# A polysketch attention feeding a SwiGLU block: key features of the third batch earlier, query features one operation per unit, weight splits later

## The chip, the cores and the metric

The kernel runs on one core of a Trainium2 chip. The metric is the device time of one execution in microseconds (us), as the median of the runs given. The profile is of one further execution, with its own time.

## The reference

Four batches of four heads, 1088 tokens of 32 numbers each. Attention has no softmax: queries and keys are turned into 64 products of two sketches of 8, keys and values are summed once per head, and every query is a product with that sum. The result (4352 tokens of 128 numbers) goes through a SwiGLU block with 1536 hidden numbers.

```python
def phi(x):
    a = np.einsum('rd,bhsd->bhsr', S1, x)
    b = np.einsum('rd,bhsd->bhsr', S2, x)
    return np.einsum('bhsi,bhsj->bhsij', a, b).reshape(*x.shape[:-1], r * r)
q_p, k_p = (phi(q), phi(k))
kv = np.einsum('bhsf,bhsd->bhfd', k_p, v)
z = np.sum(k_p, axis=2)
num = np.einsum('bhsf,bhfd->bhsd', q_p, kv)
den = np.einsum('bhsf,bhf->bhs', q_p, z)[..., None] + 1e-06
x = (num / den)          # (B,H,S,D) -> (B*S, H*D) = (4352, 128)
g = x @ w_gate           # 128 -> 1536
silu = g * (1.0 / (1.0 + np.exp(-g)))
out = silu * (x @ w_val) @ w_out
```

The inputs come in 64-bit floating point; the kernel makes 32-bit numbers of their words.

## The kernel before

The tokens lie in `xT` (128 x 4352), one column per token, and are cut into blocks: three of the first batch (384, 320, 384 tokens: blocks 0, 1, 2) and then blocks of 480 (3 and on). The hidden numbers are cut into 12 chunks of 128. A *unit* (i, j) is one block by one chunk: a gate product and a value product on PE (TensorE), a Silu on ACT (ScalarE), and a product of the two on DVE (VectorE), which leaves the hidden numbers of the unit in a slot of `hbuf` or `late`. A *down* multiplies one unit's hidden numbers with its chunk of `w_out` and adds to the block's sum in PSUM. The order of work on every engine is the order in which the program issues it: scheduling is by hand, and each engine works through its own queue in that order.

There are two kinds of units. For blocks 0, 1 and part of 2, `unit` (L1010) multiplies 32-bit numbers directly. A unit called with `late=True` does not use DVE: ACT writes Silu to `room` (L1022) and copies the value product to its slot (L1030), and the two are multiplied later on POOL (GpSimd) by `catch_up` (L1039, L1042). Otherwise DVE multiplies them at once (L1033). From unit (2, 6) on, `start_unit` (L976) and `finish_unit` (L987) work with numbers that are split in parts: `start_unit` multiplies the parts `wd` and `xd` (L982) into one of three pairs of PSUM banks and ACT rescales the pair (L985); `finish_unit` adds two more products each (L994, L995), then come Silu (L997) on ACT and the product (L1002) on DVE, after which the pair is free for a later `start_unit`.

The parts of the weights are made by `cut_weights` (L841), for three chunks at a time, in four steps: a rounded copy on ACT (L845), the rest on POOL (L848), a scaled copy of it on ACT (L850), a difference on POOL (L857). In the code `g0` is the gate weights of chunks 0 to 2, `v1` the value weights of chunks 3 to 5, and so on; `at("g0")` issues the next step. `cut_tokens` (L859) makes `x1` on ACT (L867), `xd` (L875) and `x0` (L870) of a block's tokens. `narrow` (L245) makes 32-bit weights out of the words: two operations on DVE, two on ACT (L268, L269), two on DVE (L271, L277), one on POOL (L286); `part("wv", 2)` issues the next of these steps for the value weights of chunks 3 to 5.

The attention of the first batch runs at the start: `query_products`, `query_copy` (L461), `query_features` (`phq`, L475), `totals` (L497) and `divide` (L518 to L539, which writes `xT`). The other batches are a generator, `attentions`, of which `parts_of(n)` runs the next n pieces between units or downs, up to a piece marked "pe" that `group()` runs at a fixed place in the last loop. Its pieces for a batch are: turns of keys and queries (L327, L578); key features `phk` on DVE (`features`, L377); their sums `zs` on POOL (`feature_sums`, L547, five operations); products of features and values (L388), of the next batch's keys (L354) and of the sums (L715) on PE; `fold` (L601 to L608), which puts the sum into the weights `s123`; the queries' sketches with these on PE (L342) and their copies on ACT (L590); `query_step` (L739), eight pieces: `dot` and `den` (L743, L746), the division (L748 to L750), and three times a product `phq` (L377, 768 elements) and its turn into `phT` (L760); and `numerators` (L768), whose products (L778) are copied into `xT` (L795). `phk` and `phT` share one buffer, so the key features of the third batch (index 2) can be written only when the second batch's numerators have been multiplied.

The downs between the last direct unit and unit (2, 6) are the loop over n from 0 to 12; then come units (2, 6) to (2, 11) with a down each (the loop over j), then the remaining downs (`while todo`), and then the last loop over y, 12 units for each of the blocks 3 and on. At y = 4 its first `group()` runs the third batch's sums.

Of the kernel before, what the change touches and what calls it, by code (L numbers as in the profile page):

```python
# [19 lines left out]
def kernel(  # L20
# [28 lines left out]
    nc = tc.nc  # L49
# [263 lines left out]
    late = const.tile([P, NL, BW], FP32, tag="late", name="late", bufs=1)  # L313
# [301 lines left out]
    def attentions():  # L615

        yield from turn_keys(1)
        kp = pair("keys")  # L620
        for i, c in enumerate(kpieces):
            key_products(kp[:, i, :], *c)
        ka = apool.tile([P, NC * H, R], FP32, tag="kas", name="kas")

        def sketch(ps, i):
            c0, c1 = kpieces[i]
            return ps[:, i, 0 : 64 * (c1 - c0)].rearrange("p (x t r) -> p x t r", t=2, r=R)

        for i, (c0, c1) in enumerate(kpieces):
            nc.scalar.copy(ka[:, H * c0 : H * c1, :], sketch(kp, i)[:, :, 0, :])  # L630
        yield from turn_queries(1)
        phk = apool.tile([P, NC, H, R, R], FP32, tag="phk", name="phk")
        for n, (i, c0, c1) in enumerate(((0, 0, 3), (0, 3, 5), (1, 5, 7), (1, 7, 9))):
            first = H * (c0 - kpieces[i][0])
            kb = sketch(kp, i)[:, first : first + H * (c1 - c0), 1, :]
            key_features(phk, (ka[:, H * c0 : H * c1, :], kb), c0, c1)
            if n == 0:
                zs, sums = feature_sums(phk)
            else:
                sums.pop(0)()  # L640
            if n == 3:
                let_go("keys")
            if n % 3 != 1:
                yield
        sums.pop(0)()
        yield from turn_keys(2)
        kvz = pair("values")
        key_values(kvz[:, 0, 0:F], phk, 0, NC)
        kab, copies = sketched(pair(), key_products, 2, "kab2")
        run_copies(copies, 2)  # L650
        value_sums(kvz[:, 0, :], zs)
        fold(kvz[:, 0, :])
        spread = spread_out(1, kvz[:, 0, :])
        let_go("values")
        yield
        qab, copies = sketched(pair(), query_sketches, 3, "qab")
        run_copies(copies, 2)
        yield
        for n, _ in enumerate(query_step(1, qab)):
            if n % 2 == 1:  # L660
                yield
        numerators(1, spread)
        yield "first"

        phk = apool.tile([P, NC, H, R, R], FP32, tag="phk", name="phk")
        yield from features(phk, kab)
        zs, sums = feature_sums(phk)
        for f in sums:
            f()
        yield from turn_keys(3)  # L670
        yield from turn_queries(2)
        for b in (2, 3):
            yield "pe"
            if b == 3:
                numerators(2, spread)
            kv = bank("g2")
            key_values(kv[:, 0:F], phk, 0, NC)
            if b == 2:
                kab, copies = sketched(pair(), key_products, 2, "kab2")
                run_copies(copies, 2)  # L680
            value_sums(kv, zs)
            fold(kv)
            spread = spread_out(b, kv)
            yield
            yield "pe"
            qab, copies = sketched(pair(), query_sketches, 3, "qab")
            run_copies(copies, 2)
            yield
            if b == 2:
                yield from turn_queries(3)  # L690
                phk = late[:, NL - 6 :, :].rearrange("p s (n h i j) -> p (s n) h i j", h=1, i=R, j=R)
                phk = phk.rearrange("p (c h) o i j -> p c (h o) i j", h=H)
                yield from features(phk, kab)
                zs, sums = feature_sums(phk)
            yield from beside(query_step(b, qab), sums)
        yield "pe"
        numerators(3, spread)
        yield
# [40 lines left out]
    def query_step(b, qab):  # L739
        phT = turned[b] = apool.tile([P, H, 2, NC, 32], FP32, tag="phk", name="phT")  # L740
        dot = apool.tile([P, NC * H, R], FP32, tag="dot", name="dot")
        den = apool.tile([P, NC * H], FP32, tag="den", name="den")
        nc.vector.tensor_tensor(  # L743
            out=dot[:], in0=qab[:, 1, :, :], in1=qab[:, 2, :, :], op=ALU.mult
        )
        nc.vector.tensor_reduce(out=den[:], in_=dot[:], axis=AX.X, op=ALU.add)  # L746
        yield
        nc.vector.tensor_scalar_add(den[:], den[:], 1e-6)  # L748
        nc.vector.reciprocal(den[:], den[:])
        nc.vector.tensor_tensor(  # L750
            out=qab[:, 0, :, :], in0=qab[:, 0, :, :],
            in1=den[:].unsqueeze(2).to_broadcast([P, NC * H, R]), op=ALU.mult,
        )
        yield
        for c0, c1 in fpieces:
            x, n = slice(H * c0, H * c1), c1 - c0
            phq = apool.tile([P, NC // 3, H, R, R], FP32, tag="phqs", name="phq")
            key_features(phq, (qab[:, 0, x, :], qab[:, 1, x, :]), 0, n)
            yield
            nc.vector.transpose(  # L760
                out=phT[:, :, :, c0:c1, :].rearrange("p h g c t -> p c (h g) t"),
                in_=phq[:, 0:n, :, :, :].rearrange(
                    "p c h (g i) j -> p c (h g) (i j)", g=2
                ),
            )
            yield
# [32 lines left out]
    HEAD = len(steps)  # L799
    hidden = {}  # L800
    acc = {}
    todo = []
# [207 lines left out]
    def unit(i, j, late=False, between=(None, None), apart=False):  # L1010


        t0, n = blocks[i]
        g, u = halves(pair()) if apart else (bank(), bank())
        for o, w in ((g, wg), (u, wv)):
            if between[0] and w is wv:
                between[0]()
            nc.tensor.matmul(  # L1018
                o[:, 0:n], w[:, j, :], xT[:, t0 : t0 + n], start=True, stop=True
            )  # L1020
        sg = room[:, len(lates) + caught[0], :] if late else fpool.tile([P, WB], FP32, tag="sg", name="sg", bufs=5)
        nc.scalar.activation(sg[:, 0:n], g[:, 0:n], AF.Silu)  # L1022
        slot_of[i, j] = slots.pop(0)
        hj = slot_of[i, j]
        hidden[i, j] = hj
        todo.append((i, j))
        if late:
            if between[1]:
                between[1]()
            nc.scalar.copy(hj[:, 0:n], u[:, 0:n])  # L1030
            lates.append((hj[:, 0:n], sg[:, 0:n]))
        else:
            nc.vector.tensor_tensor(  # L1033
                out=hj[:, 0:n], in0=sg[:, 0:n], in1=u[:, 0:n], op=ALU.mult
            )
# [146 lines left out]
    n = steps[0][1]  # L1182
# [50 lines left out]
    def parts_of(n):  # L1233

        for _ in range(n):
            if ahead[0] not in ("pe", "end"):
                ahead[0] = next(att, "end")
# [21 lines left out]
    qbs = [query_copy(steps[2][1], *ps) for ps in pss]  # L1259
    part("wv", 2)  # L1260
    part("wg", 2)
    unit(1, 1, late=True)
    phq = query_features(steps[2][1], pss, qbs)
    part("wv", 2)
    for _ in range(3):
        catch_up()
    unit(1, 2, late=True)
    nd = totals(steps[2][1], phq, kvz, side_by_side("a"))
    divide(0, *steps[2], nd)

# [25 lines left out]
    def at(*names):  # L1296
        for name in names:
            next(cuts[name], None)

    def next_down():  # L1300
        if order:
            todo.remove(order[0])
            todo.insert(0, order.pop(0))
        down()

    steps_at = {20: ("v2",), 21: ("v3", "v2", "v3"), 22: ("g2",), 23: ("g3",)}
    for z, (i, j) in enumerate(seq):
# [15 lines left out]

    steps_at = {
        0: ("g2", "v2", "v3"), 1: ("g2",), 2: ("g2", "g3"), 3: ("g3", "v2"), 4: ("g3", "v3"), 5: ("g2",),
        7: ("x",), 8: ("x", "v0"), 9: ("g3", "v1"), 10: ("g0",), 11: ("g1",),
    }
    ND = 13
    for n in range(ND):
        if n == ND - 2:  # L1330
            start_unit(2, 6)
        next_down()
        parts_of(n in (0, 1, 5, 8, 10, 12))
        at(*steps_at.get(n, ()))
        if n in (5, 6, 7):
            catch_up()


    steps_at = {
        6: ("v0", "v1", "g0"), 7: ("g1", "v0", "v1"), 8: ("g0", "g1", "v0"), 9: ("v1", "g0"), 10: ("g1",),  # L1340
    }
    todo.sort(key=lambda x: (order + [x]).index(x))
    for j in range(6, NCH):
        if j + 1 < NCH:
            start_unit(2, j + 1)
        finish_unit(2, j)
        next_down()
        parts_of(j in (6, 8))
        at(*steps_at.get(j, ()))
    parts_of(1)  # L1350
    x_steps = cut_tokens(HEAD, nc.vector, soon=True)
    while todo:
        if len(todo) == 2:
            start_unit(HEAD, 0)
        next_down()
        next(x_steps, None)

    flat = hbuf[:].rearrange("p s w -> p (s w)")
    slots[:] = [flat[:, WB * k : WB * k + WB] for k in range((NH - NL) * BW // WB)]
# [72 lines left out]
```

## Time and profile before

| | us |
|---|---|
| median of 3 runs | 283.14 |
| lowest and highest run | 283.03, 284.88 |
| profiled execution, whole | 283.87 |
| profiled execution, span | 282.1 |
| PE busy in the span | 270.7 (96%) |
| DVE busy | 206.9 (73%) |
| ACT busy | 189.7 (67%) |
| POOL busy | 105.9 (38%) |

The span is the part of the execution that the trace shows. Times in the trace count from the span's start. A 32-bit product on PE is shown as two records whose shown ends overlap the next one, so the distance from start to start is what a product takes there: a direct unit of 384 tokens takes 1.29 us (L1018 at 28.08 and again at 29.37).

### The profile page before, as it was taken

What the parts mean: (1) busy time and instruction counts of PE and PEld (TensorE: products, weight loads), DVE (VectorE), ACT (ScalarE), POOL (GpSimd) and SP (SyncE); (2) the same over time, 40 slices, a digit from 0 to 9 for tenths busy, and PEclk for the clock granted to TensorE, in tenths of its full rate; (3) what the DMA queues carried; (4) which work ended last, traced back from release to release, by engine and by line L of the source; (5) the groups of instructions that cost most, each with busy time, mean ns of one, the idle gap of its engine ahead of it and who ended that gap; (6) DMA issues with size and microseconds to landing.
All of it is one profiled execution on the core that took longest, in us unless ns stands there. A gap on an engine that the chain in (4) does not pass through costs nothing.

```text
span 282.1 us, 5723 instructions
## 1 busy us (share of the span) xinstructions
PE 270.7 (96%) x2181; PEld 200.0 (71%) x2181; DVE 206.9 (73%) x353; ACT 189.7 (67%) x337; POOL 105.9 (38%) x114
## 2 busy tenths in 40 slices
PE   7999999998989969999999999999999999999995
PEld 6645566666765747677667777767887788788994
DVE  2997988799895393688745667867996995988431
ACT  2468566462683555766748898869879888886860
POOL 3314422169990072071005543533435362633000
PEclk9999999999999999999999999999999999999999
DMA  6573195223221103300200001000200200010021
GB/s 192 162 217 96 34 277 177 81 79 90 53 65 26 28 2 94 81 1 0 35 7 12 0 13 26 0 2 3 33 0 2 35 0 1 11 26 0 6 32 28
DMA packets 26139, 14.30 MB, mean 51 GB/s; under 512 B 19840, under 2 KB 24192, under 8 KB 26112
## 3 DMA queue, kind: packets, MB, share of 16 engines
q1 hardware_dynamic: 25456, 13.84, 19.3%
q8 instruction: 17, 0.28, 0.4%
q10 hardware_dynamic: 656, 0.10, 0.2%
q14 instruction: 10, 0.08, 0.1%
HBM read 11.41 MB, written 2.23 MB: 48 GB/s over the span
## 4 chain that ended last, share of the span: by engine, by line
PE 83%; DVE 7%; POOL 4%; issue 2%; DMA 2%; ACT 1%; SPq 0%; POOLq 0%; DVEq 0%; ACTq 0%
PE PS L1070 19%; PE PS L994 13%; PE PS L982 13%; PE PS L995 12%; PE PS L1018 11%; POOL zs L547 4%; PE PS L1065 2%; PE PS L1062 2%; PE PS L1064 2%; PE PS L778 2%; PE PS L342 2%; DMA kld<-in_k_dram 2%; DVE hbuf L1002 1%; DVE phq L377 1%; PE PS L1098 1%
## 5 line engine op out<-in xcount | busy, mean ns | idle before, releaser
L985 ACT ACTIVATE PS<-PS 128x960 f32<-128x960 f32 (+1 forms) x90 | 83.3, 926 | 37.0 <-PE PS L982 36.0
L1002 DVE SCALAR_TENSOR_TENSOR hbuf<-PS,sg 128x480 f32<-128x480 f32 (+1 forms) x87 | 55.2, 636 | 43.3 <-ACT sg L997 40.8
L997 ACT ACTIVATE sg<-PS 128x480 f32<-128x480 f32 (+1 forms) x90 | 49.6, 551 | 2.6 <-ACT sg L997 1.3
L1070 PE MATMUL PS<-hbuf,wo 128*128 128x480 f32 (+3 forms) x118 | 46.4, 490 | 0.0
L982 PE MATMUL PS<-xd,graw 128*128 128x480 f32 (+1 forms) x69 | 38.3, 556 | 0.0
L982 PE MATMUL PS<-xd,wd 128*128 128x480 f32 (+1 forms) x90 | 33.8, 376 | 1.0 <-DVE hbuf L1002 1.0
L995 PE MATMUL PS<-x,wb 128*128 128x480 f32 (+1 forms) x90 | 33.5, 372 | 0.0
L994 PE MATMUL PS<-x,w 128*128 128x480 f32 (+1 forms) x90 | 33.4, 371 | 0.0
L1070 PEld LDWEIGHTS PS<-hbuf,wo 128*128 128x128 f32 x118 | 21.8, 189 | 5.7 <-issue 0.9
L982 PEld LDWEIGHTS PS<-xd,wd 128*128 128x128 f32 x90 | 17.0, 189 | 12.2 <-issue 6.0
L995 PE MATMUL PS<-x,graw 128*128 128x480 f32 (+1 forms) x69 | 25.5, 370 | 0.0
L1018 PE MATMUL PS<-xT,wg 128*128 128x384 f32 (+1 forms) x60 | 23.5, 474 | 0.1
L1018 PE MATMUL PS<-xT,wv 128*128 128x384 f32 (+1 forms) x60 | 23.2, 467 | 0.3 <-DVE wv L286 0.3
L870 POOL TENSOR_TENSOR x<-xT,x 128x480 fp32r<-128x480 f32 (+1 forms) x6 | 7.2, 1194 | 37.4 <-ACT x L867 37.4
L1022 ACT ACTIVATE sg<-PS 128x384 f32<-128x384 f32 (+1 forms) x24 | 11.2, 468 | 13.2 <-PE PS L1018 12.4
L982 PEld LDWEIGHTS PS<-xd,graw 128*128 128x128 f32 x69 | 13.0, 188 | 7.7 <-ACT PS L985 4.0
L994 PEld LDWEIGHTS PS<-x,w 128*128 128x128 f32 x90 | 16.9, 187 | 2.2
L995 PEld LDWEIGHTS PS<-x,wb 128*128 128x128 f32 x90 | 16.9, 188 | 2.1
L994 PE MATMUL PS<-x,graw 128*128 128x480 f32 (+1 forms) x48 | 18.4, 383 | 0.0
L1070 PE MATMUL PS<-hbuf,scaled 128*128 128x480 f32 x36 | 17.4, 564 | 0.0
L962 POOL TENSOR_TENSOR hlate<-hbuf,hlate 128x480 fp32r<-128x480 f32 x10 | 12.9, 1291 | 9.8 <-ACT hlate L961 7.7
L1018 PEld LDWEIGHTS PS<-xT,wv 128*128 128x128 f32 x60 | 11.2, 190 | 7.4 <-DVE hbuf L1033 0.8
(196 smaller groups left out, 544.9 us busy)
## 6 DMA issues: line engine op xcount, KB each, us to landing
kld<-in_k_dram SPq DMA_DIRECT2D x4, 544.0 KB, 4.8
vld<-in_v_dram SPq DMA_DIRECT2D x12, 144.0 KB, 4.2
qld<-in_q_dram SPq DMA_DIRECT2D x3, 544.0 KB, 3.4
raw<-in_moe_w_out_dram SPq DMA_DIRECT2D x4, 384.0 KB, 5.1
raw<-in_moe_w_gate_dram SPq DMA_DIRECT2D x3, 384.0 KB, 3.6
raw<-in_moe_w_val_dram SPq DMA_DIRECT2D x3, 384.0 KB, 3.9
out_dram<-o SPq DMA_DIRECT2D x16, 60.0 KB, 1.9
vld<-in_v_dram SPq DMA_DIRECT2D x4, 112.0 KB, 4.0
```

The source lines that it names most:

```text
L547: add = lambda o, a, b: nc.gpsimd.tensor_tensor(out=o, in0=a, in1=b, op=ALU.add)
L870: engine.tensor_tensor(out=x0[:, 0:n], in0=x, in1=whole(x1[:, 0:n]), op=ALU.subtract)
L962: add_to(before, y + 2, lambda: nc.gpsimd.tensor_tensor(out=h0, in0=h, in1=whole(h1), op=ALU.subtract))
L982: nc.tensor.matmul(ps[:, k], w_parts[id(w), j // 3][2][:, j % 3, :], xd, start=True, stop=True)
L985: nc.scalar.activation(ps, ps, AF.Copy, scale=-1.0 / WHOLE)
L994: nc.tensor.matmul(ps[:, k], w1, x1, start=False, stop=False, skip_group_check=True)
L995: nc.tensor.matmul(ps[:, k], wb, x0, start=False, stop=True, skip_group_check=True)
L997: nc.scalar.activation(sg, ps[:, 0], AF.Silu, scale=WHOLE)
L1002: nc.vector.scalar_tensor_tensor(out=hj[:, 0:n], in0=ps[:, 1], scalar=WHOLE, in1=sg, op0=ALU.mult, op1=ALU.mult)
L1018: nc.tensor.matmul(o[:, 0:n], w[:, j, :], xT[:, t0 : t0 + n], start=True, stop=True)
L1022: nc.scalar.activation(sg[:, 0:n], g[:, 0:n], AF.Silu)
L1070: nc.tensor.matmul(acc[i][:, 0:n], w, hidden[i, j][:, 0:n], **sides)
```

## The change

Three things are changed, all of them in the order of issue or in the form of a unit; the products on PE are the same in number.

Units (1, 1) and (1, 2) are no longer `late`: their Silu goes to an `sg` buffer and DVE multiplies at once (L1033). Two `catch_up` calls of the three that stood in the loop over n fall away.

`query_step(1)` hands back after every piece instead of every second, and the places of `parts_of` are moved: the third piece of the attention in that loop (products, `fold`) from n = 5 to n = 7, the query sketches from 8 to 10, and then one piece of `query_step` at each of n = 11, n = 12 and j = 6 to 11. The second batch's numerators follow when seven downs are left, three downs later than before; with four and fewer left, the third batch's key features, their sums and the turns of the next keys are issued, which stood at y = 0 to 3 before.

The cut of block 2's tokens comes at n = 6 and 7 (7 and 8 before). The splits `v0`, `g0`, `v1`, `g1` are spread from n = 8 to the last downs, where they stood at n = 8 to j = 10.

```diff
@@ attentions
-        for n, _ in enumerate(query_step(1, qab)):
-            if n % 2 == 1:
-                yield
+        yield from query_step(1, qab)
         numerators(1, spread)
@@
-    unit(1, 1, late=True)
+    unit(1, 1)
     phq = query_features(steps[2][1], pss, qbs)
     part("wv", 2)
     for _ in range(3):
         catch_up()
-    unit(1, 2, late=True)
+    unit(1, 2)
     nd = totals(steps[2][1], phq, kvz, side_by_side("a"))
     divide(0, *steps[2], nd)
@@
-        7: ("x",), 8: ("x", "v0"), 9: ("g3", "v1"), 10: ("g0",), 11: ("g1",),
+        6: ("x",), 7: ("x",), 8: ("g3", "v0"), 9: ("g0",), 10: ("v0",), 11: ("g0",),
     }
@@
-        parts_of(n in (0, 1, 5, 8, 10, 12))
+        parts_of(n in (0, 1, 7, 10, 11, 12))
         at(*steps_at.get(n, ()))
-        if n in (5, 6, 7):
+        if n == 5:
             catch_up()
@@
-        6: ("v0", "v1", "g0"), 7: ("g1", "v0", "v1"), 8: ("g0", "g1", "v0"), 9: ("v1", "g0"), 10: ("g1",),
+        6: ("v0",), 7: ("g0",), 8: ("v1",), 9: ("g1",), 10: ("v0",), 11: ("g0", "v1"),
@@ for j in range(6, NCH)
-        parts_of(j in (6, 8))
+        parts_of(1)
         at(*steps_at.get(j, ()))
-    parts_of(1)
-    x_steps = cut_tokens(HEAD, nc.vector, soon=True)
+    x_steps = iter(())
+    steps_at = {9: ("g1",), 8: ("v1",), 6: ("g1",), 4: ("v1", "g1")}
     while todo:
         if len(todo) == 2:
             start_unit(HEAD, 0)
         next_down()
+        at(*steps_at.get(len(todo), ()))
         next(x_steps, None)
+        if len(todo) == 7:
+            parts_of(1)
+            x_steps = cut_tokens(HEAD, nc.vector, soon=True)
+            next(x_steps)
+        if len(todo) < 5:
+            parts_of(1)
```

## The prediction

> **What bounds the kernel now.** I read first the page's busy times and its slices, then the table of stretches of 4 us, then the waits, then the timeline of the stretches that the change touches.
>
> ```profile
> PE 270.7 (96%) x2181; PEld 200.0 (71%) x2181; DVE 206.9 (73%) x353; ACT 189.7 (67%) x337; POOL 105.9 (38%) x114
> PE   7999999998989969999999999999999999999995
> ...
> 68.00:72.00 4.00, 3.15 (x64) 2.16 (x64) 3.91 (x9) 1.53 (x4) 3.92 (x5) 1.00 0.64 177
> 76.00:80.00 4.00, 3.74 (x19) 3.08 (x18) 3.90 (x4) 3.51 (x7) 4.00 (x4) 1.00 0.56 148
> 80.00:84.00 4.00, 3.27 (x16) 2.62 (x16) 3.93 (x6) 3.04 (x7) 4.00 (x4) 1.00 0.00 0
> 100.00:104.00 4.00, 2.38 (x91) 1.75 (x91) 4.00 (x7) 1.66 (x3) 3.84 (x3) 1.00 0.00 0
> 104.00:108.00 4.00, 2.58 (x43) 2.16 (x39) 2.29 (x6) 1.59 (x3) 3.18 (x4) 1.00 0.41 130
> ```
>
> PE is the bound: from 24 us on every stretch but these five (and 3.92 at 188) shows 4.00 until 276. Their gaps are 0.85, 0.26, 0.73, 1.62 and 1.42, together 4.88 us: the most that the change can win, as it moves PE's products but takes none away. The timeline names what ends each gap (columns: start, duration, engine, line, in brackets the idle time before).
>
> ```profile
> 69.14 0.32 PE L715 MATMUL PS<-zs,ones 128*32 128x64 f32 x8 [0.85 <-POOL zs L547]
> 79.20 0.44 PE L982 MATMUL PS<-xd,wd 128*128 128x384 f32 x1 [0.26 <-DVE hbuf L1002]
> 81.78 0.44 PE L982 MATMUL PS<-xd,wd 128*128 128x384 f32 x1 [0.73 <-DVE hbuf L1002]
> 99.93 1.58 POOL L547 TENSOR_TENSOR zs<-phk 128x512 f32<-128x512 f32 x1 [15.18 <-DVE phk L377]
> 100.50 0.99 PE L388 MATMUL PS<-phk,vld 128*32 128x64 f32 x56
> 106.22 0.32 PE L715 MATMUL PS<-zs,ones 128*32 128x64 f32 x8 [1.42 <-POOL zs L547]
> ```
>
> The third batch's sums start when DVE has made its key features between two units, and PE arrives before they end. From 100.50 to the next L982 at 106.47 pass 5.97 us for products that take 2.65 where nothing is late (65.87, 1.15 of L388, 1.27 of L354, 0.25 of L715): 3.3 us are waits.
>
> The other place is the start, where PE has no gap:
>
> ```profile
> 24.18 1.02 DVE L475 TENSOR_TENSOR phq<-PS,qb 128x384 f32<-128x384 f32 x2 [0.67 <-ACT qb L461]
> 25.34 0.45 ACT L1022 ACTIVATE room<-PS 128x320 f32<-128x320 f32 x1
> 25.88 0.88 PE L497 MATMUL PS<-phq,kvz 64*32 64x192 f32 x32
> 26.22 1.00 POOL L286 TENSOR_TENSOR wv<-man,exp 128x384 f32<-128x384 f32 x1 [1.63 <-DVE man L277]
> 27.44 0.81 PE L1018 MATMUL PS<-xT,wv 128*128 128x384 f32 x2
> ```
>
> The reader is to see the slack: phq ends at 25.20 and `totals` follows at 25.88 because PE is busy until then; the value weights of chunks 3 to 5 are ready at 27.22, and the product that needs them, of unit (0, 3), starts at 27.44. There is 0.7 us of slack in the one and nearly none in the other.
>
> **What the Trainium skill says.** "PSUM — Partial Sum Buffer", section "Engine vs sequencer instructions": the queues of ScalarE, VectorE and GpSimd are strict first in, first out. The trace agrees: DVE is idle 0.67 us ahead of L475, with nothing behind it taken first. "SBUF — State Buffer", section "SBUF: two separate sides": VectorE (with two SBUF inputs) and GpSimd share a pair of ports as an exclusive lock, held for a whole instruction. The trace agrees: `dot` (L743) takes 0.46 us with POOL free, and 1.22 when it starts at 153.72, inside a POOL operation that lasts from 153.60 to 154.62. Products with a PSUM input don't show it (L1002 of 480 is 0.65 or 0.66 whether POOL works or not). So I price phq, phk, xd and x0 at their free time and add what is left of the POOL operation that they run into.
>
> **Part 1: units (1, 1) and (1, 2) at once on DVE.** Removed: two copies on ACT (0.45, 0.47) and two products on POOL (1.13 each, 3.39 for three). All lie beside PE, so they bring nothing. Added: two L1033 of 320 elements (0.45 to 0.49). The first stands in DVE's queue ahead of the two L475, and it waits for Silu of (1, 1). ACT has worked without a pause since 22.28 (copies, `qb`, the words' steps), and none of that is taken from ahead of it, so Silu still ends at 25.34 + 0.45 = 25.79. Hence L1033 at 25.83, both L475 at 26.30 and 26.77, done at 27.32 (before 25.20). `totals` can do a quarter of its 0.81 on the first half; the rest, 0.61, follows 27.37 and ends at 27.98 instead of 26.69: 1.3 us late. Behind L475 stand L271 and L277 of the value weights: L277 ends at 28.28 (before 26.14), L286 runs on POOL from 28.36 to 29.36, and the product of (0, 3) follows at 29.58 instead of 27.44: 2.1 us late. Before, PE lost 0.28 in unit (0, 5) (start to start 1.57 us, not 1.29, on L1033 behind `divide`); with PE later that wait is covered: `divide` runs from 28.62, 2.81 as before, to 31.4, and L1033 ends at 31.9, ahead of the product at 32.2. Loss: 2.14 - 0.28 = 1.9 us at unit (2, 0). Bounds: 1.3 (only `totals` late) and 2.3 (a POOL catch-up caught by `divide`). From there to 68 us PE shows no gap that could take it back: between 30.94 and 61.37 lie 12 units of 384 at 1.29, 9 of 320 at 1.08, 6 downs at 0.64 and one L354 at 1.2, in all 30.2 of 30.4 us. All that follows starts 1.9 us later. Below I keep to the clock of before, and take the 1.9 off at the end.
>
> **Part 2: products and sketches two downs later.** The value sums come after two more downs of 320 (0.54 each), at 69.37, when `zs` (done at 69.09) is there: the 0.85 goes. But xd (L875) now stands ahead of `fold` on DVE. It runs into POOL's two wd operations (69.05, 2.27 for both) and ends at 70.9; `fold` and what follows take 0.9 (69.53 to 70.44) and run into the second wd: `s123` is ready at 71.8 to 72.2. PE, after its three downs, is there at 71.3 and waits. L342 from 72.2 takes 1.6, so `start_unit(2, 6)` comes at 73.8, against 73.77. I count nothing for this part (bounds 0 and +0.85).
>
> **Part 3: one operation of the query features per unit, splits spread out.** A unit with its down takes PE 1.59 us (75.19 to 76.78). DVE gets 0.52 (L1002) and then a phq (0.95) or a turn (0.98): 1.5 us, or more with the lock. ACT gets 0.71 + 0.37 + 0.45, which is 1.53. Both fit, so the waits at 79.20 and 81.78 (1.0 us) go. What is late next is the last turn. L1002 of (2, 6) can't come before its Silu ends at 77.3, and from there DVE has six L1002 (0.46 from start to start), three phq, three turns (0.9) and one output turn (0.45): 2.8 + 2.6 + 2.7 + 0.45 = 8.6, and 1 to 2 us of lock waits, now that single splits on POOL meet each phq: 87 to 88. PE gets to the numerators after three more downs at 86.9, so they start at about 87.4 and end, 1.5 later, at 88.9. Before they ended at 87.93 with those three downs (0.65 each) still to do, which is 89.87. Gain: 1.0 us (bounds 0.4 and 1.4).
>
> **Part 4: key features behind the numerators.** Five downs (3.1 us) cover the copies, x1 and xd; `start_unit(3, 0)` comes at 92.0 (before 92.90). DVE has after 88.9: the copy, a wait until x1 ends at 90.4 (as before, 1.5 after the numerators), xd and x0 to 91.6, one POOL split (wd of `g1`) that phk or x0 runs into, 1.0, then phk of 768 (0.86) and three of 512 (0.60 each) with zs' first sum (1.28) between the last two or not, keys' turn 0.7, output turn 0.52, keys' turn 0.65, and only now L1002 of (3, 0), a query turn 0.72, L1002 of (3, 1). That one ends at 99.1 without the 1.28 and at 100.4 with it; before:
>
> ```profile
> 97.07 0.66 DVE L1002 SCALAR_TENSOR_TENSOR hbuf<-PS,sg 128x480 f32<-128x480 f32 x1 [1.37 <-ACT sg L997]
> 98.51 0.65 DVE L1002 SCALAR_TENSOR_TENSOR hbuf<-PS,sg 128x480 f32<-128x480 f32 x1
> 99.22 0.48 PE L982 MATMUL PS<-xd,wd 128*128 128x480 f32 x1
> ```
>
> The second one frees the bank that PE needs at 99.22. PE would be there at 98.2 now, but waits for DVE: 99.15 to 100.45, middle 99.8, and has finished unit (3, 3) 1.28 later, at 101.1 (before 100.50). The 1.0 us of part 3 is thus lost here, with 0.6 more.
>
> **Part 5: the sums.** phk is done before 97, zs (four more sums, 1.28 twice and 0.72 twice, with locks) by 101 to 102; PE asks for them at 101.1 + 2.4. So the group takes 2.65 and the next L982 comes at 103.75 instead of 106.47. Gain 2.7 (bounds 2.1 and 3.4). From y = 4 on all queues stand in the same order as before and PE is the bound to the end.
>
> **Sum.** 2.7 - 1.9 = 0.8 us gained: a span of 281.3, an execution of 283.1 where the profiled one took 283.87 (1.77 around its span). That one lies 0.73 above the median; on the median, 283.14 - 0.8 = 282.3.
>
> **Rivals.**
> - The gaps go and nothing else comes: the added L1033 are hidden, DVE is in time everywhere. For it: the units' two operations together take less than PE, and DVE has 27% idle. Against it: ACT was shown to hold Silu until 25.79. It gives 283.14 - 4.9 = 278.2; with the early loss alone absent, 283.14 - 2.7 = 280.4.
> - Slower: DVE behind the numerators. L1002 of (3, 0) stands behind two tokens' parts, four key features and three turns, each of which may lose a lock to POOL. It decides from where L1002 of (3, 1) ends later than 100.55 on the clock of before: then PE is at L982 later than 106.47 - 1.9. With the last turn at 88.2, as the locks of part 3 allow, and zs' sum between, it ends at 101.5: 1.0 us slower, 284.1. For it: the 1.66 and 1.76 us of phq at 75.97 and 82.12 in place of 0.95. Against it: POOL has only one split left behind the numerators.
> - The gain is all eaten at the start and in part 2 (L342 late by more than 0.9, wv weights late by 2.3): no change, 283.1.
>
> **How the numbers follow.** Chances: forecast 0.50; no change 0.14; the slower rival 0.22; nothing lost 0.12; something unseen 0.02. The range takes in the slower rival, and on the fast side part 5's upper bound with the lesser early loss (3.4 - 1.3 = 2.1, and some way to 280.4): 280.5 to 284.6. 1% is 2.83 us, about what a measurement of this kernel can tell from no change, so faster means below 280.31: the first rival in most of its forms, 0.13. Slower means above 285.97, which needs two more us of locks than the slower rival: 0.09. The rest, 0.78, lies within 1%.
>
> **What would show it.** Right: in the profile after, PE has a gap of about 1.3 us ahead of L497 near 26 us and one ahead of the wv product behind it; L715 of the third batch has no wait for zs; L982 of units (3, 3) and (3, 4) waits for L1002; L778 waits for the last turn. Wrong: no gap near 27 us would take part 1 away, and then a time near 280.4; no waits for L1002 at 96 to 102 would add another 1 us of gain. If L715 still waited for zs, POOL would be the step that I had too early.

## The result and the profile after

The changed kernel takes 281.63 us (median of 20 runs, 281.39 to 283.27), the kernel before 283.21 (20 runs): the ratio is 0.9934 with a 95% interval of 0.9913 to 0.9954, a gain of 1.6 us or 0.7%. The forecast was a gain of 0.8 and a time of 282.3. The time lies inside the range that was given with it (280.5 to 284.6), but 0.8 lies outside the measured interval, which is a gain of 1.3 to 2.5 us.

The first 22 us are issued alike in all kernels here, yet they differ by up to 2 us from execution to execution: the row L445 at 22.66 before stood at 21.85 to 23.93 in the traces of this study. Two things differ in them. The first turn of keys on DVE starts at 5.32 to 6.13, when the keys have landed; and in the traces of the first three experiments PE's first products take longer (36 records of L354 in 2.19 or 1.89 us, where the others show 1.49), after which L445 comes 17.8 us behind that turn and not 16.5. I therefore count places from the row L445 when I compare traces. Lines below `query_step` carry numbers that are smaller by 2 in the changed kernel: L1000 is what L1002 was, L980 is L982, L1068 is L1070, L713 is L715.

The page's busy times and PE's slices:

```profile
PE 269.9 (97%) x2181; PEld 199.7 (71%) x2181; DVE 208.6 (75%) x355; ACT 188.9 (68%) x335; POOL 102.7 (37%) x112
PE   7898999999999889999999999999999999999995
```

The stretches of 4 us in which PE is below 4.00 between 24 us and 184 (columns: length, then busy time and count of PE, PEld, DVE, ACT, POOL, then clock and DMA):

```profile
24.00:28.00 4.00, 3.04 (x39) 1.40 (x37) 2.99 (x7) 1.30 (x4) 0.56 (x1) 1.00 0.25 91
28.00:32.00 4.00, 3.69 (x12) 2.19 (x12) 3.86 (x9) 1.42 (x3) 3.31 (x4) 1.00 0.36 98
72.00:76.00 4.00, 3.67 (x81) 2.84 (x80) 2.77 (x6) 1.83 (x3) 3.63 (x4) 1.00 0.23 41
84.00:88.00 4.00, 3.78 (x45) 2.25 (x44) 3.48 (x5) 0.90 (x2) 1.54 (x1) 1.00 0.25 41
96.00:100.00 4.00, 2.31 (x10) 1.68 (x10) 4.00 (x8) 2.21 (x4) 3.76 (x4) 1.00 0.23 37
```

None of the five gaps of before is left. There are five others: 0.96, 0.31, 0.33, 0.22 and 1.69. The timeline of the changed kernel names what ends each:

```profile
26.11 1.23 PE L497 MATMUL PS<-phq,kvz 64*32 64x192 f32 x32 [0.96 <-DVE phq L475]
28.49 0.91 PE L1016 MATMUL PS<-xT,wv 128*128 128x384 f32 x2 [0.31 <-POOL wv L286]
72.70 1.69 PE L342 MATMUL PS<-s,qT 128*32 128x96 f32 x72 [0.33 <-DVE s L608]
87.53 1.57 PE L776 MATMUL PS<-phT,spread 32*32 32x288 f32 x64 [0.22 <-DVE phT L758]
98.82 0.48 PE L980 MATMUL PS<-xd,wd 128*128 128x480 f32 x1 [1.70 <-DVE hbuf L1000]
103.76 0.32 PE L713 MATMUL PS<-zs,ones 128*32 128x64 f32 x8
```

The last row is the third batch's sum, which waited before and does not now. The first five are the new waits. How the time stands at five places, from the row L445 of each trace (the forecast is the prediction's place against that of the kernel before):

| place on PE | before | after | difference | forecast |
|---|---|---|---|---|
| unit (2, 0) starts | 8.28 | 9.97 | +1.69 | +1.9 |
| unit (2, 6) starts | 51.11 | 52.48 | +1.37 | +1.9 |
| unit (3, 0) starts | 70.24 | 70.21 | -0.03 | +1.0 |
| products of the third batch's keys (L388) | 77.84 | 79.57 | +1.73 | +2.5 |
| next unit's first product | 83.81 | 82.16 | -1.65 | -0.8 |

The change loses 1.7 us at the start, wins it back up to the numerators, loses it a second time in the first units of block 3, and wins 3.4 us at once where the sums are no longer late.

### The profile page after: what moved, and what is told of

The parts are those of the page before. It is cut to its first block, busy times and chain, and to the rows that moved or that the text cites. A ratio compares the mean times of both kernels' runs of the same rounds, so it can differ in the third digit from the quotient of the medians.

```text
span 279.7 us, 5723 instructions
## 1 busy us (share of the span) xinstructions
PE 269.9 (97%) x2181; PEld 199.7 (71%) x2181; DVE 208.6 (75%) x355; ACT 188.9 (68%) x335; POOL 102.7 (37%) x112
## 4 chain that ended last, share of the span: by engine, by line
PE 80%; DVE 12%; ACT 2%; issue 2%; DMA 1%; POOL 0%; SPq 0%; DVEq 0%; ACTq 0%
PE PS L1068 16%; PE PS L992 13%; PE PS L980 13%; PE PS L993 13%; PE PS L1016 10%; PE PS L1060 2%; PE PS L1063 2%; PE PS L1062 2%; PE PS L776 2%; PE PS L342 2%; DVE phk L377 2%; DMA kld<-in_k_dram 1%; PE PS L354 1%; PE PS L388 1%; DVE phT L758 1%
## 5 line engine op out<-in xcount | busy, mean ns | idle before, releaser
L1000 DVE SCALAR_TENSOR_TENSOR hbuf<-PS,sg 128x480 f32<-128x480 f32 (+1 forms) x87 | 55.2, 634 | 42.9 <-ACT sg L995 40.3
L1068 PE MATMUL PS<-hbuf,wo 128*128 128x480 f32 (+3 forms) x118 | 45.8, 488 | 0.0
L980 PE MATMUL PS<-xd,graw 128*128 128x480 f32 (+1 forms) x69 | 38.2, 554 | 0.0
L980 PE MATMUL PS<-xd,wd 128*128 128x480 f32 (+1 forms) x90 | 33.5, 372 | 1.7 <-DVE hbuf L1000 1.7
L1068 PEld LDWEIGHTS PS<-hbuf,wo 128*128 128x128 f32 x118 | 22.0, 189 | 5.6 <-issue 0.4
L980 PEld LDWEIGHTS PS<-xd,wd 128*128 128x128 f32 x90 | 17.0, 189 | 12.2 <-issue 5.8
L1020 ACT ACTIVATE sg<-PS 128x384 f32<-128x384 f32 (+1 forms) x26 | 11.9, 466 | 15.7 <-PE PS L1016 14.8
L980 PEld LDWEIGHTS PS<-xd,graw 128*128 128x128 f32 x69 | 13.0, 188 | 7.7 <-ACT PS L983 4.1
L1068 PE MATMUL PS<-hbuf,scaled 128*128 128x480 f32 x36 | 17.4, 564 | 0.0
```

The source lines that it names most:

```text
L980: nc.tensor.matmul(ps[:, k], w_parts[id(w), j // 3][2][:, j % 3, :], xd, start=True, stop=True)
L1000: nc.vector.scalar_tensor_tensor(out=hj[:, 0:n], in0=ps[:, 1], scalar=WHOLE, in1=sg, op0=ALU.mult, op1=ALU.mult)
L1068: nc.tensor.matmul(acc[i][:, 0:n], w, hidden[i, j][:, 0:n], **sides)
```

## The experiments

**The two units late again.** The changed kernel without its first part:

```diff
-    unit(1, 1)
+    unit(1, 1, late=True)
...
-    unit(1, 2)
+    unit(1, 2, late=True)
...
-        if n == 5:
+        if n in (5, 6, 7):
             catch_up()
```

> The changed kernel with units (1, 1) and (1, 2) late again and all three catch-ups in the loop over n; everything else as changed. Theory (the two direct units cost PE about 1.7 us at the start, because DVE waits for their Silu ahead of the query features): the wait of 0.96 us ahead of L497 near 26 us and the one ahead of the wv product behind it go, unit (2, 0) starts 1.6 to 1.7 us earlier, and the time falls by 1.4 to 1.7 us, from about 281.5 to 279.8 to 280.1. Rival (the loss at the start is taken back later, where DVE sets the pace behind the numerators): the earlier start is lost again before y = 4, the time stays at 281.5 within 0.4. Second rival (the relief of ACT and POOL matters more): slower than the changed kernel, 282 or more.

279.98 us, ratio to before 0.9879 (0.9854 to 0.9904), so 1.6 us less than the changed kernel. The waits at L497 and at the wv product are gone: from L445 (23.64) to unit (2, 0) (31.92) it is 8.28 us again. The loss at the start is real and is taken back nowhere: the numerators come 63.92 us behind L445 here and 65.68 in the changed kernel.

**The two units alone**, on the kernel before:

```diff
-    unit(1, 1, late=True)
+    unit(1, 1)
...
-    unit(1, 2, late=True)
+    unit(1, 2)
...
-        if n in (5, 6, 7):
+        if n == 5:
             catch_up()
```

> The kernel before with only units (1, 1) and (1, 2) made direct and two catch-ups less; nothing else of the change. Theory (a loss of 1.7 us at the start that nothing takes back): 283.1 + 1.7 = 284.8, with waits of PE ahead of L497 and of the wv product of unit (0, 3). Rival (the two products less on POOL let the splits and sums come earlier and pay for it): 283.1 to 283.6.

286.62 us, ratio 1.0111 (1.0074 to 1.0148): 3 us, not 1.7. From L445 to the third batch's sums it is 86.10 us, against 83.56 before: 2.5 more belong to the change, and the rest to the spread of the first 22 us (three of the six runs lie at 285.7 to 285.9). The start is as expected, with waits of 0.97 and 0.31 and 1.69 us up to unit (2, 0). The rest is lost where units (2, 9) and (2, 10) are started, whose waits were 0.26 and 0.73 before:

```profile
82.49 0.44 PE L982 MATMUL PS<-xd,wd 128*128 128x384 f32 x1 [0.54 <-DVE hbuf L1002]
85.59 0.44 PE L982 MATMUL PS<-xd,wd 128*128 128x384 f32 x1 [1.24 <-DVE hbuf L1002]
```

That is 0.79 more. In the trace the second phq takes 1.72 us, not 1.20: it starts at 82.35, just behind a POOL operation for `wd` from 82.25, where before it started at 79.07, ahead of the one from 79.42. With two catch-ups less on POOL its splits meet other DVE operations. This reading of the 0.79 is argued from the trace, and no run isolates it. In the traces the first part costs more in the old order of work (2.5) than in the new one (1.8). (From 108 to 112 us of this trace the granted TensorE clock was 0.73. The distance from L354 to the sums, 2.68, is still that of before, 2.69, so the 2.5 does not come from it.)

**The product behind the query features.** The unit stays direct; only the place of its DVE product in the queue moves, behind the query features and behind the last two steps of the value weights on DVE.

```diff
+            def product():
+                nc.vector.tensor_tensor(
+                    out=hj[:, 0:n], in0=sg[:, 0:n], in1=u[:, 0:n], op=ALU.mult
+                )
...
-    unit(1, 1)
+    products = []
+    unit(1, 1, after=products)
     phq = query_features(steps[2][1], pss, qbs)
     part("wv", 2)
+    products.pop()()
```

> The changed kernel with the direct product of unit (1, 1) issued on DVE behind the query features and the last DVE step of the value weights, not ahead of them; the unit stays direct. Theory (not the extra DVE work but its place costs: first in, first out behind a Silu that is late): PE no longer waits at L497, and 1.3 to 1.7 us come back, 279.8 to 280.2. Rival (the work of two more DVE products in a busy stretch costs, wherever they stand): less than 0.5 us comes back, 281.0 to 281.5.

280.01 us, ratio 0.9875 (0.9850 to 0.9901): the whole 1.6 us come back, with the same extra work on DVE. DVE's timeline (L1032 here is L1031 in the changed kernel):

```profile
25.19 1.02 DVE L475 TENSOR_TENSOR phq<-PS,qb 128x384 f32<-128x384 f32 x2 [0.67 <-ACT qb L461]
26.13 0.55 DVE L271 SCALAR_TENSOR_TENSOR exp<-raw,exp 128x384 int32<-128x384 int32 x1
26.59 0.55 DVE L277 SCALAR_TENSOR_TENSOR man<-raw,man 128x384 f32<-128x384 uint32 x1
27.06 0.88 DVE L1032 TENSOR_TENSOR hbuf<-sg,PS 128x320 f32<-128x320 f32 x2
```

In the changed kernel the first of these products stood ahead, and DVE stood still for it:

```profile
25.01 0.49 DVE L1031 TENSOR_TENSOR hbuf<-sg,PS 128x320 f32<-128x320 f32 x1 [2.30 <-ACT sg L1020]
25.41 1.01 DVE L475 TENSOR_TENSOR phq<-PS,qb 128x384 f32<-128x384 f32 x2
```

The reader is to compare the brackets: 2.30 us of idle time for Silu, against 0.67 for `qb`. It is the place, not the work. And with 279.98 for the late units and 280.01 for the direct ones in this place, the first part of the change brings nothing even where it costs nothing.

**The turns in the last loop again.** Only the four key features stay behind the numerators:

```diff
-        if len(todo) < 5:
+        if 2 <= len(todo) < 5:
             parts_of(1)
```

> The changed kernel with only the key features behind the numerators; the sums' issue and the two turns of the next keys stand in the last loop again (from y = 0 on), behind the first product L1002 (L1000 in the changed kernel). Theory (the turns ahead of the product of unit (3, 0) hold the PSUM bank that PE waits for, 1.70 us at 98.8): that wait falls to about 0.4, the unit of y = 3 ends 1.3 us earlier, and the time falls to about 280.2. Rival (the sums on POOL or the keys' turns then end last, and L713 or L354 waits instead): a gain under 0.4, 281.1 to 281.5.

280.28 us, ratio 0.9889 (0.9861 to 0.9916), 1.35 us less than the changed kernel. DVE and PE at unit (3, 0) and its bank, in the changed kernel and then here:

```profile
92.57 3.85 DVE L377 TENSOR_TENSOR phk<-kab 128x768 f32<-128x768 f32 x4
96.34 0.83 DVE L327 STREAM_TRANSPOSE kT<-kld 128x640 f32<-128x640 f32 x1
97.10 0.53 DVE L1110 STREAM_TRANSPOSE o<-PS 128x384 f32<-128x384 f32 x1
97.56 0.66 DVE L327 STREAM_TRANSPOSE kT<-kld 128x512 f32<-128x512 f32 x1
98.16 0.61 DVE L1000 SCALAR_TENSOR_TENSOR hbuf<-PS,sg 128x480 f32<-128x480 f32 x1
```

```profile
96.32 0.57 DVE L1110 STREAM_TRANSPOSE o<-PS 128x384 f32<-128x384 f32 x1
96.82 0.61 DVE L1000 SCALAR_TENSOR_TENSOR hbuf<-PS,sg 128x480 f32<-128x480 f32 x1
97.36 0.82 DVE L327 STREAM_TRANSPOSE kT<-kld 128x640 f32<-128x640 f32 x1
...
97.48 0.49 PE L980 MATMUL PS<-xd,wd 128*128 128x480 f32 x1 [0.37 <-DVE hbuf L1000]
...
102.42 0.32 PE L713 MATMUL PS<-zs,ones 128*32 128x64 f32 x8
```

The two turns no longer stand ahead of the product that frees the bank; the wait is 0.37 in place of 1.70, and the sums are still in time. That wait is what the change paid for getting the sums early, and it did not have to.

**Both moves.** The edits of the last two kernels together.

> The changed kernel with both moves: the product of unit (1, 1) behind the query features on DVE, and the keys' turns in the last loop again. Theory (two waits at two places, each a delay of all that follows, so that they add): 281.5 - 1.5 - 1.25 = 278.7, within 0.3. Rival (they share a cause, DVE's total work in the first 100 us, and do not add): 279.5 to 280.

278.73 us (4 runs), ratio 0.9823 (0.9791 to 0.9854). The two gains add, as expected: 2.9 us less than the changed kernel.

**The cut of block 2's tokens one down later**, in the kernel with both moves:

```diff
-        6: ("x",), 7: ("x",), 8: ("g3", "v0"), 9: ("g0",), 10: ("v0",), 11: ("g0",),
+        7: ("x",), 8: ("x", "g3", "v0"), 9: ("g0",), 10: ("v0",), 11: ("g0",),
```

> The kernel with both moves, and the cut of block 2's tokens one down later (at n = 7 and 8, as before the change), so that fold stands ahead of xd on DVE. Theory (L342 waits 0.33 us for fold behind xd, and behind a POOL split that its last product runs into): that wait goes and the time falls by 0.2 to 0.4 against the kernel with both moves, 278.3 to 278.5. Rival (the query features, not PE, set the numerators' start, and x0 now stands ahead of them): no change within 0.15, or slower.

278.14 us (4 runs), ratio 0.9802 (0.9771 to 0.9834), 0.16 below the range that was expected. L342 no longer waits: from L445 to L342 it is 48.70 us here and 49.09 with both moves alone, and the numerators keep that distance (63.53 and 63.92): 0.39 won. The medians differ by 0.59, and the intervals overlap, so that this step rests on one trace of each kernel. This is the fastest kernel of the study, 2.0% below the kernel before (1.7 to 2.3).

**The query features in pairs.** The changed kernel with `query_step` handing back after every second piece:

```diff
-        yield from query_step(1, qab)
+        for n, _ in enumerate(query_step(1, qab)):
+            if n % 2 == 1:
+                yield
...
-        parts_of(n in (0, 1, 7, 10, 11, 12))
+        parts_of(n in (0, 1, 7, 10, 12))
...
-        parts_of(1)
+        parts_of(j in (7, 9, 11))
         at(*steps_at.get(j, ()))
```

> The changed kernel with query_step handing back after every second piece again (at n = 12 and j = 7, 9, 11), so that a product phq and its turn stand together between two products L1000 (L1002 here) on DVE. Theory (two operations of 1.9 us together exceed the 1.6 us of a unit, one does not): PE waits for the unit product at L982 (0.2 to 1 us) and for the last turn at L778 (1 us in place of 0.22), 282.3 to 282.8. Rival (the order within a few units does not matter, since the sum of DVE's work is the same): 281.5 within 0.3.

283.31 us, ratio 0.9981 (0.9966 to 0.9995), 1.7 us more than the changed kernel and above the range that I gave. PE waits at two places, and DVE shows the pair that holds the unit's product:

```profile
80.03 1.80 DVE L377 TENSOR_TENSOR phq<-qab 128x768 f32<-128x768 f32 x1
81.93 0.98 DVE L760 STREAM_TRANSPOSE phT<-phq 128x768 f32<-128x768 f32 x1
82.83 0.52 DVE L1002 SCALAR_TENSOR_TENSOR hbuf<-PS,sg 128x384 f32<-128x384 f32 x1
...
83.41 0.44 PE L982 MATMUL PS<-xd,wd 128*128 128x384 f32 x1 [0.54 <-DVE hbuf L1002]
89.50 1.57 PE L778 MATMUL PS<-phT,spread 32*32 32x288 f32 x64 [1.02 <-DVE phT L760]
```

The numerators start 1.62 us later, from L445, than in the changed kernel, and all that follows keeps that distance. So the order within a few units does matter, but this run changes two things at once. The first phq is issued a unit later and starts 57.83 us behind L445, not 56.25; from there to the end of the last turn DVE takes as long as in the changed kernel (9.41 and 9.38 us), and so do the three phq (4.23 and 4.17). The 1.62 are thus the later start. The pair itself shows in the wait of 0.54 for the unit's product, and without it PE would, by these figures, only have waited longer for the last turn. A run with pairs that begin as early was not made.

**The key features in the last loop.** The changed kernel with its last part undone:

```diff
-        if len(todo) < 5:
-            parts_of(1)
```

> The changed kernel with the third batch's key features, sums and turns in the last loop (y = 0 to 4), where they stood before the change; numerators, query features and splits as changed. Theory (moving them removed 3.3 us of waits at L388, L354 and L713, and put 1.7 us of a new wait at the unit product in their place): the waits of the kernel before come back, 3.0 to 3.3 us, the wait of 1.70 us goes, and the time rises by 1.3 to 1.7 to about 283. Rival (POOL's splits, spread out in front of the sums, decide): the sums end earlier or later than 5.0 us after the first key feature and the time moves by another amount, below 282.3 or above 284.

284.11 us, ratio 1.0012 (0.9991 to 1.0034), no better than before, and about 1 us above what was expected. PE's waits at the third batch:

```profile
101.47 0.43 PE L388 MATMUL PS<-phk,vld 128*32 128x64 f32 x16 [0.63 <-DVE phk L377]
102.88 1.27 PE L354 MATMUL PS<-s,kT 128*64 128x64 f32 x36 [0.98 <-DVE kT L327]
105.56 0.32 PE L713 MATMUL PS<-zs,ones 128*32 128x64 f32 x8 [1.41 <-POOL zs L547]
```

They are those of the kernel before (0.64, 0.98, 1.42), 3.0 us in all; the wait of 1.70 is not there. From L445 the sums come at 83.52 here and at 81.91 in the changed kernel, so the move brings 1.6 us. In the kernel before the sums come at 83.56: without its last part the change wins just what it loses at the start.

Seven of this kernel's 14 runs lie at 283.1 to 283.6 us and seven at 284.6 to 285.3. Of the changed kernel's 20 runs only four lie in such an upper group (283.1 to 283.3), so the medians differ by more than 1.6. That the groups are the spread of the first 22 us fits the traces (the two executions of the first and third experiments with L445 at 23.6 are the slowest of their kernels) but is not shown for each run.

The median lies where the rival had put it, above 284, but the trace speaks against the rival: the sums end 8.50 us after the first key feature starts, and 8.51 in the kernel before. (The 5.0 of the expectation is neither.)

No run isolates the spread of the weight splits, or the later place of the value sums and the sketches. What is said of these below is read from the traces.

## Why the prediction was right

The direction was right, and so were the places where time is won and lost and, but for one product in part 4, the waits behind them. The size was not: the gain was 1.6 where I gave 0.8. That the time fell inside the range says little, since the range was wide enough for a loss.

- **Part 1** (1.9 us lost, bounds 1.3 and 2.3): 1.69. Silu's end, counted from L445, was right to a hundredth: the added product started 3.16 us behind L445 where 3.17 was worked out. The weights on POOL were 0.11 earlier than worked out and the product behind them 0.28, since I carried the 0.22 us between POOL's end and PE's product over from a place where PE was still busy with the product ahead; where PE waits it is 0.05. That `divide` no longer holds unit (0, 5) was right.
- **Part 2** (0, bounds 0 and +0.85): 0.32 won. `fold` stood behind xd as said, and L342 waited 0.33 for it; I had it wait 0.9.
- **Part 3** (0.9 won up to unit (3, 0)): 1.40. Both waits for unit products went, and the last turn set the numerators' start, as said, but with 0.22 us of waiting where I had 0.5. The locks were right: the three phq took 1.80, 1.44 and 0.93, which is 1.3 over their free time, where I had 1 to 2. Two terms ahead of and beside them were too large. Silu of (2, 6) ended 3.27 us after its unit's start, where I had 3.5, and from there to the end of the last turn passed 9.88 us, where I had about 10.1.
- **Part 4** (1.5 lost, from 0.9 ahead to 0.6 behind): 1.76. The cause was right, DVE late with a unit's product, but the sum has it one unit too late: I had taken the product of (3, 1) as the one that decides, and it was that of (3, 0), for whose bank PE waited in unit (3, 3) until 98.82. The second ended at 100.06, ahead of PE at 100.24, so that the size came out near for a wait at another product. The key features met POOL's first sum, as I had it for the late end: the four took 3.85 us where free ones would take 2.7.
- **Part 5** (3.3 won): 3.38. L713 came with zs ready, 3.2 us after its last sum ended. This is the part that the gain rests on.

The errors of my terms are 0.2 + 0.3 + 0.5 in the first three parts, all on one side, less 0.3 in part 4 and with 0.1 from part 5: 0.8, the whole difference. They are small, but nearly all lie on one side, and the forecast was a small difference of large terms. The 4.88 us that I took as the most that could be won were a little low as well: the gaps in the brackets are shorter than what is lost (at the third batch 0.64, 0.98 and 1.42 make 3.04, where the distances give 3.3).

The rival in which nothing is lost falls with the first and fourth experiments, which each find one of the two losses. The slower rival had its mechanism right (DVE behind the numerators) but its condition was not met: L1000 of (3, 1) ended at 99.18 on the clock of before with the loss at the start taken off, where by the prediction it decides from 100.55.

## What to carry to other kernels

A short operation that waits for a busy engine can cost far more than its own time, since all that stands behind it in the same queue waits too (here a product of 0.49 us cost 1.6): ask of every added operation when its last input is there, and put it behind the work that can run sooner. When a chain is moved forward, move only the links that are late (here four products) and leave those that were in time (two turns) behind the operation that frees what the bounding engine needs next. Price a chain of waits on a bound engine at each place it passes, since a gain made upstream can be lost at the next operation that another engine holds back (here 1.4 us won and 1.8 lost again).

## What was not expected of the hardware

Work taken away from POOL went with a slower DVE: with two POOL products less, the three phq took 5.12 us in the second experiment and 4.62 before, and PE waited 0.79 us more beside them. The traces suggest that the lock works out by which of DVE and POOL comes first at that moment; no run isolates it. As the prediction had priced it, an operation with a PSUM input kept its time beside POOL: L1000 of 384 elements took 0.51 to 0.56 us in the changed kernel, whether POOL worked (83.0, 0.54) or not (77.6, 0.56), while phq from SBUF alone went from 0.93 to 1.80.
